# Two early loads of one column of Wa and of Wb, and a causal table that GpSimd builds behind seven of its DMA issues

## The chip, the cores and the metric

The kernel runs on one core of a Trainium2 chip. The metric is the device time of one execution in microseconds (us). Before the change it is 124.75 us, the median of three runs (124.61 to 125.31).

The core's engines are PE (matrix products), DVE (VectorE), ACT (ScalarE), POOL (GpSimd) and SP (SyncE, which here only issues DMA transfers). Each follows its own list of instructions in order, and they wait for one another by semaphores.

## The reference

Two stages follow one another. The first is a chunked state-space scan over 4 batches, 8 heads, 768 tokens, head width 32 and state width 16:

```python
cum = np.cumsum(log(a), axis=-1)                 # within a chunk of 32 tokens
L = np.exp(cum[..., :, None] - cum[..., None, :]) * causal
M = np.einsum('bhin,bhjn->bhij', C, B) * L
y = np.einsum('bhij,bhjd->bhid', M, x)           # within the chunk
y += np.einsum('bhin,bhnd->bhid', C, state) * exp(cum)
state = exp(sum(log a)) * state + sum_j(B_j x_j exp(cum_last - cum_j))
```

The second is a bilinear feed-forward layer on the result, 3072 tokens of width 256, with weights of 256 x 1536, 256 x 1536 and 1536 x 256:

```python
out = ((X @ w_a) * (X @ w_b)) @ w_out
```

## The kernel before

The kernel works with chunks of 128 tokens, six blocks of them along the sequence (`NBLK`), and takes two batches at a time. Block and batch pair give 12 **pairs** (`p` from 0 to 11). For a pair it loads B, C and x; scales B and C by the running products of `a` (`scale_bc`, giving `bm` and `cm`); turns both on PE (`transposes`); forms the scores (`scores`, into the PSUM tiles SC0 and SC1); multiplies them with a causal table of zeros and ones (`mask`, line 426 on DVE or lines 423 and 424 through ACT and POOL); multiplies the result with the scaled x (`pv_u`, line 447) and makes the state's share (`ds_mm`, line 474). The output goes to X2T (later pairs: XB), the left operand of the feed-forward layer. That layer's products with Wa and Wb go to PSUM tiles `aps` and `bps`; ACT copies `aps` to `asb` (line 639) and DVE multiplies `bps` by it into `hk` (line 646).

The order on every engine is written out by hand (`manual_schedule`): an engine does its instructions in the order in which the program's text gives them. There is no planner. PSUM banks of the feed-forward products are handed out by the string `BANKS`.

What touches the change:

- **The inputs of pair 0** are loaded first (lines 183 to 194), in pieces, alternating between SP's and ACT's DMA queues: `a`, B, C, a small table `ch`, then x. Of pair 0's x (256 KB), 192 KB go through ACT's queue and 64 KB through SP's.
- **The inputs of pair 1**: half of its x is issued by SP (`x1`, line 203), and a hand-made dependency holds this issue until DVE has made `fB` of pair 0 (line 761). B, C and the other half of x are issued by POOL (lines 215 and 218).
- **The weights** are float32 in memory and float16 on the chip, and POOL issues their transfers (`load_w`, line 171). Wa and Wb are each held in two tiles of 768 columns, `W[0]` and `W[1]`. Their first tiles come in two transfers each, one for rows 0 to 127 (`f` = 0) and one for rows 128 to 255 (`f` = 1): Wa at lines 216 and 217, Wb at 219 and 220. The second tiles follow later, one transfer for each weight.
- **The tables**: DVE fills `ident`, `causal` and `causal_q` with ones, and POOL's `affine_select` sets the unwanted elements to zero. `ident` (line 205) is the identity for the transposes. `causal` (line 210, in two halves of 64 partitions) is the mask of pairs 0 to 3, and its first reader is DVE's first masked product of pair 0 (line 426).
- **PE's first feed-forward work** is on pair 0 and comes between the parts of pair 1: three `aps` products on Wa (`units_mm`, line 628), with the scores of pair 1 in between; then four matmuls on Wb's first half, then the second product of pair 1 (line 447), its state share (line 474), and the rest on Wb (line 628). From then on whole units (`unit`, line 615) alternate with the pairs' work.

DMA issues on SP and ACT share eight completion semaphores in turn, and POOL's have eight others. An issue that takes a semaphore over waits for the transfer that used it before.

The piece of text around the change, shortened:

```python
x1 = load1(nc.sync, 1, 2, 0)
...
for w in range(2):
    for bt in range(2):
        load1(nc.gpsimd, 1, w, bt)
load_w(Wa, 0, 0)
load_w(Wa, 0, 1)
load1(nc.gpsimd, 1, 2, 1)
load_w(Wb, 0, 0)
load_w(Wb, 0, 1)
```

Of the kernel before, what the change touches and what calls it, by code (L numbers as in the profile page):

```python
# [10 lines left out]
f32 = mybir.dt.float32  # L11
# [3 lines left out]
ALU = mybir.AluOpType  # L15
# [14 lines left out]
def kernel(  # L30
# [13 lines left out]
    nc = tc.nc  # L44
# [3 lines left out]
    Q = 128  # L48
# [28 lines left out]
    causal = const.tile([128, 2, Q], f16, name="causal")  # L77
# [5 lines left out]
    big = ctx.enter_context(tc.tile_pool(name="big", bufs=1))  # L83
# [10 lines left out]
    maskbd = big.tile([128, H, D], f16, name="maskbd")  # L94
    warm = big.tile([128, 128], f16, name="warm")
    causal_q = big.tile([128, Q], f16, name="causal_q")
    Pr = big.tile([BH, NBLK, Q], f32, name="Pr")
    rmid = big.tile([BH, NBLK], f32, name="rmid")
    NE = P0 // NBP
# [43 lines left out]
    def by_token(t_):  # L143
        return t_.rearrange("p h r n -> p (h r n)").rearrange("p (t h n) -> p t h n", t=2, h=H)

    def load1(eng, p, which, bt, i0=0, n=64):
        blk, bp = divmod(p, NBP)
        if p >= P0:
            return eng.dma_start(
                by_token(pair_in[p][which])[:, bt],  # L150
                (B, C, x)[which][2 * bp + bt, :, blk * Q : (blk + 1) * Q, :].rearrange("h q n -> q h n"),
            )
        src = (B, C, x)[which][2 * bp + bt, :, blk * Q + 2 * i0 : blk * Q + 2 * i0 + 2 * n, :]
        return eng.dma_start(
            pair_in[p][which][64 * bt + i0 : 64 * bt + i0 + n].rearrange("i h r n -> i h (r n)"),
            src.rearrange("h (i r) n -> i h (r n)", r=2),
        )
# [10 lines left out]
    def load_w(W, t, f=None):  # L168
        src = (moe_w_a if W is Wa else moe_w_b).rearrange("(f p) e -> p f e", p=128)[:, :, t * KC : (t + 1) * KC]
        fs = slice(0, 2) if f is None else slice(f, f + 1)  # L170
        return nc.gpsimd.dma_start(W[t][:, fs], src[:, fs])
# [12 lines left out]
    for p_ in range(3):  # L184
# [7 lines left out]
    load1(nc.scalar, 0, 2, 1)  # L192
    load1(nc.sync, 0, 2, 0, 0, 32)
    load1(nc.scalar, 0, 2, 0, 32, 32)
    nc.scalar.preload_act_table_set("natural_log_exp_and_others")
    nc.gpsimd.memset(warm.bitcast(u32), 0)
    nc.vector.memset(ident, 1.0)
# [7 lines left out]
    nc.gpsimd.affine_select(  # L205
        out=ident, in_=ident, compare_op=ALU.is_equal, fill=0.0, base=0, pattern=[[-1, 128]], channel_multiplier=1
    )
    for bt in range(2):
        v = causal[64 * bt : 64 * bt + 64]
        nc.gpsimd.affine_select(  # L210
            out=v, in_=v, compare_op=ALU.is_ge, fill=0.0, base=0, pattern=[[-1, 2], [1, Q]], channel_multiplier=-2
        )
    for w in range(2):
        for bt in range(2):
            load1(nc.gpsimd, 1, w, bt)
    load_w(Wa, 0, 0)
    load_w(Wa, 0, 1)
    load1(nc.gpsimd, 1, 2, 1)
    load_w(Wb, 0, 0)
    load_w(Wb, 0, 1)  # L220

# [531 lines left out]
    def pull(p):  # L753
# [33 lines left out]
        out=causal_q, in_=causal_q, compare_op=ALU.is_ge, fill=0.0, base=0, pattern=[[1, Q]], channel_multiplier=-1  # L787
# [30 lines left out]
    for bt in range(2):  # L818
# [14 lines left out]
        out=hsx[0:BH],  # L833
# [246 lines left out]
```

## Time and profile before

| what | value |
|---|---|
| median of three runs | 124.75 us |
| the profiled execution's own time | 125.11 us |
| its span, from first to last instruction | 123.40 us |
| PE busy | 117.3 us, 95% |
| DVE busy | 91.0 us, 74% |
| ACT busy | 75.7 us, 61% |
| POOL busy | 61.2 us, 50% |
| moved by DMA | 12.15 MB, 99 GB/s over the span |
| granted PE clock | full in all 40 slices |

The profile is of one execution, so its span is compared with its own time: 1.71 us lie before and behind the span. A line number such as L628 is a line of the kernel before. In the timeline a row gives start, duration, engine, line, operation and tiles; consecutive instructions of one kind are merged, and "xn" counts them. Rows of DMA issues on SP, ACT and POOL say how long the issue took, not the transfer; the time from issue to landing is listed apart. The chain of waits is followed back from the last instruction: at each step to what released it.

Some landings that the text uses, in us from the span's start: `a` at 2.9; pair 0's B at 3.3 and 4.25, its C between 4.7 and 5.1, its x between 7.3 and 7.6; pair 1's B at 5.5 and 6.8, its C at 7.8 and 8.0, its x at 11.8 (SP) and 12.3 (POOL).

### The profile page before, as it was taken

How to read it: one execution, taken by the hardware profiler on the slowest of the kernel's cores; microseconds unless marked ns; L12 is line 12 of the kernel's file. 1: busy time of each engine (PE TensorE's matmuls, PEld its weight loads, DVE VectorE, ACT ScalarE, POOL GpSimd, SP SyncE). 2: the span in 40 equal slices, each digit the busy share in tenths (PEclk: the TensorE clock that was granted, in tenths of full speed). 3: DMA queues.
4: the chain of work that ended last, by engine and by line, in shares of the span. 5: the costliest groups of instructions: out<-in, count | busy, mean ns of one | idle time of the engine just before them, and what ended most of it. 6: DMA issues, size and time to landing. Idle time of an engine off the chain costs nothing.

```text
span 123.4 us, 3704 instructions
## 1 busy us (share of the span) xinstructions
PE 117.3 (95%) x1456; PEld 80.0 (65%) x1456; DVE 91.0 (74%) x182; ACT 75.7 (61%) x158; POOL 61.2 (50%) x88
## 2 busy tenths in 40 slices
PE   6799799999999999999999999999999999999990
PEld 2345669889898798744477465757464775555890
DVE  3999598973995979799986988996889544747200
ACT  0447846837669866987669767457637746657220
POOL 7997989099492994097996970056000000000000
PEclk9999999999999999999999999999999999999999
DMA  3999999978899989799977601011101012010122
GB/s 66 195 155 210 185 198 204 164 137 77 89 125 115 108 111 103 91 118 93 129 271 169 204 5 45 5 43 45 43 0 43 5 43 88 0 48 0 43 85 85
DMA packets 56401, 12.15 MB, mean 99 GB/s; under 512 B 51168, under 2 KB 55936, under 8 KB 56384
## 3 DMA queue, kind: packets, MB, share of 16 engines
q1 hardware_dynamic: 51808, 7.43, 36.3%
q0 software_dynamic: 2304, 4.06, 17.4%
q10 hardware_dynamic: 2272, 0.43, 1.8%
q8 instruction: 11, 0.18, 0.6%
q14 instruction: 6, 0.05, 0.1%
HBM read 11.13 MB, written 3.15 MB: 116 GB/s over the span
## 4 chain that ended last, share of the span: by engine, by line
PE 85%; DMA 7%; DVE 5%; issue 1%; ACT 0%; DVEq 0%
PE ops L718 17%; PE aps L693 17%; PE bps L693 16%; PE ops L661 9%; PE aps L615 8%; PE bps L615 7%; DMA Wb<-in_moe_w_b_dram 5%; PE SC L372 2%; PE SC L432 2%; PE tr L342 2%; DMA a_sb<-in_a_dram 2%; DVE hk L646 1%; PE bps L628 1%; PE SC L447 1%; PE SC L522 1%; DVE fC L246 1%
## 5 line engine op out<-in xcount | busy, mean ns | idle before, releaser
L639 ACT COPY asb<-aps 128x512 f32<-128x512 f32 x72 | 41.9, 587 | 16.0 <-PE aps L693 10.4
L703 DVE TENSOR_TENSOR hkb<-bps,asb 128x512 f16<-128x512 f32 x48 | 32.3, 688 | 11.8 <-ACT asb L639 10.4
L693 PE MATMUL aps<-XB,Wa 128*128 128x512 f16 x96 | 28.6, 379 | 0.0
L693 PE MATMUL bps<-XB,Wb 128*128 128x512 f16 x96 | 28.5, 379 | 0.0
L718 PE MATMUL ops<-Wo,hkb 128*128 128x256 f16 (+1 forms) x204 | 22.8, 267 | 0.0
L718 PEld LDWEIGHTS <-hkb 128*128 128x128 f16 x204 | 18.4, 98 | 3.0
L426 DVE TENSOR_TENSOR t<-SC,causal_q 128x512 f16<-128x512 f32 x27 | 17.3, 681 | 2.2 <-PE SC L372 2.2
L646 DVE TENSOR_TENSOR hk<-bps,asb 128x512 f16<-128x512 f32 x24 | 15.6, 681 | 3.5 <-ACT asb L639 2.1
L693 PEld LDWEIGHTS <-Wb 128*128 128x128 f16 x96 | 9.9, 103 | 11.0 <-issue 0.2
L693 PEld LDWEIGHTS <-Wa 128*128 128x128 f16 x96 | 9.7, 104 | 9.2 <-issue 0.3
L730 ACT ACTIVATE osb<-ops 128x256 f32<-128x256 f32 (+1 forms) x16 | 6.0, 376 | 12.7 <-PE ops L718 12.6
L615 PE MATMUL bps<-X2T,Wb 128*128 128x256 f16 x84 | 12.6, 273 | 0.1
L615 PE MATMUL aps<-X2T,Wa 128*128 128x256 f16 x84 | 12.5, 273 | 0.2 <-DVE hk L646 0.2
L305 POOL TENSOR_SCALAR x<-xn 128x512 f16<-128x512 f32 x8 | 11.9, 1489 | 0.7
L661 PE MATMUL ops<-Wo,hk 128*128 128x256 f16 x96 | 11.7, 273 | 0.0
L661 PEld LDWEIGHTS <-hk 128*128 128x128 f16 x96 | 9.0, 98 | 1.2
L615 PEld LDWEIGHTS <-Wb 128*128 128x128 f16 x84 | 8.5, 103 | 1.1 <-issue 0.5
L615 PEld LDWEIGHTS <-Wa 128*128 128x128 f16 x84 | 8.4, 104 | 1.2 <-issue 0.5
L424 POOL TENSOR_TENSOR t<-tmp,causal_q 128x512 f16<-128x512 f32 x5 | 5.8, 1156 | 6.2 <-ACT tmp L423 6.1
L426 DVE TENSOR_TENSOR t<-SC,causal 128x512 f16<-128x512 f32 x13 | 8.2, 678 | 0.3 <-PE SC L387 0.2
L595 POOL TENSOR_TENSOR spair<-U,ch 128x128 f16<-128x128 f32 x8 | 3.1, 398 | 10.3 <-DVE U L579 10.3
L346 ACT ACTIVATE bt<-tr,ch 128x256 f16<-128x256 f16 x16 | 6.7, 472 | 0.5 <-PE tr L342 0.5
(101 smaller groups left out, 136.1 us busy)
## 6 DMA issues: line engine op xcount, KB each, us to landing
out_dram<-osb SPq DMA_DIRECT2D x23, 128.0 KB, 1.8
xn<-in_x_dram SPq DMA_DIRECT2D x5, 256.0 KB, 4.6
cn<-in_C_dram SPq DMA_DIRECT2D x8, 128.0 KB, 4.3
bn<-in_B_dram SPq DMA_DIRECT2D x8, 128.0 KB, 4.7
Wo<-in_moe_w_out_dram POOLq DMA_DIRECT2D x2, 384.0 KB, 5.9
xn<-in_x_dram POOLq DMA_DIRECT2D x3, 256.0 KB, 4.8
Wa<-in_moe_w_a_dram POOLq DMA_DIRECT2D x2, 192.0 KB, 5.5
xn<-in_x_dram SPq DMA_DIRECT2D x3, 128.0 KB, 3.5
```

The lines of the kernel that those rows point to most:

```text
L305: eng.tensor_scalar(xo, xi, XS, None, ALU.mult)
L346: b_.append(nc.scalar.activation(out=o_, in_=TB, func=AF.Copy, scale=par[:, e : e + 1]))
L424: nc.gpsimd.tensor_tensor(out=o_, in0=tmp, in1=c_, op=ALU.mult)
L426: nc.vector.tensor_tensor(out=o_, in0=i_, in1=c_, op=ALU.mult)
L615: nc.tensor.matmul(ps[:, kk * 2 * Q : (kk + 1) * 2 * Q], w_up(W, k, f), X2T[:, p, :, f], start=(f == 0), stop=(f == 1), skip_group_check=True,
L639: (nc.vector.tensor_copy if on_dve else nc.scalar.copy)(asb, a_ps)
L646: nc.vector.tensor_tensor(out=s["hk"][:, 2 * k2 : 2 * k2 + 2, :].rearrange("p k q -> p (k q)"), in0=b_ps, in1=asb, op=ALU.mult)
L661: nc.tensor.matmul(o_ps[:, 0:d_model], hk[:, k, bt * Q : (bt + 1) * Q], Wo[:, k, :], start=(k == 0), stop=(k == NK - 1), skip_group_check= ...
L693: nc.tensor.matmul(t_, w_up(W, k, f), XB[:, blk - P0 // NBP, f].rearrange("p t j q -> p (t j q)"), start=(f == 0), stop=(f == 1), skip_gro ...
L703: return lambda: nc.vector.tensor_tensor(out=s["hk"][:, k], in0=ps[1], in1=asb, op=ALU.mult)
L718: nc.tensor.matmul(o_ps[:, 0:w], hk[:, k, c * Q : (c + 1) * Q], Wo[:, k, cs], start=(k == 0), stop=(k == NK - 1), skip_group_check=True,)
L730: nc.scalar.activation(out=o_sb[:, 0:w], in_=o_ps[:, 0:w], func=AF.Copy, scale=1.0 / (YS * YS))
```

## The change

Two things are changed, both before the first product. A new tile `first` of 128 x 2 float32 takes column 0 of rows 0 to 127 of Wa and of Wb, one element a partition, in two transfers on SP's queue; they stand behind the last piece of pair 0's x and ahead of the first x of pair 1. Nothing reads the tile. And the two `affine_select` operations that finish `causal` move down POOL's list: they stood ahead of its first DMA issue, and now stand behind the issues of pair 1's B and C, of Wa's first tile and of pair 1's x, and ahead of those of Wb.

```diff
+    first = big.tile([128, 2], f32, name="first")
...
     load1(nc.sync, 0, 2, 0, 0, 32)
     load1(nc.scalar, 0, 2, 0, 32, 32)
+    for t_, W in enumerate((moe_w_a, moe_w_b)):
+        nc.sync.dma_start(first[:, t_ : t_ + 1], W[0:128, 0:1])
     nc.scalar.preload_act_table_set("natural_log_exp_and_others")
...
-    for bt in range(2):
-        v = causal[64 * bt : 64 * bt + 64]
-        nc.gpsimd.affine_select(
-            out=v, in_=v, compare_op=ALU.is_ge, fill=0.0, base=0, pattern=[[-1, 2], [1, Q]], channel_multiplier=-2
-        )
     for w in range(2):
         for bt in range(2):
             load1(nc.gpsimd, 1, w, bt)
     load_w(Wa, 0, 0)
     load_w(Wa, 0, 1)
     load1(nc.gpsimd, 1, 2, 1)
+    for bt in range(2):
+        v = causal[64 * bt : 64 * bt + 64]
+        nc.gpsimd.affine_select(
+            out=v, in_=v, compare_op=ALU.is_ge, fill=0.0, base=0, pattern=[[-1, 2], [1, Q]], channel_multiplier=-2
+        )
     load_w(Wb, 0, 0)
     load_w(Wb, 0, 1)
```

## The prediction

> **What bounds the kernel now.** I read the page's engine rows first: PE is busy 95% of the span, DVE 74%, ACT 61%, POOL 50%, and the granted clock is full in every slice. A change that adds no matmul can then only win where PE stands still, so I looked next at where the chain of waits leaves PE. From 0 to 17 us it reads (start, us, what; whole lines, others left out):
>
> ```profile
> 2.98 0.42 DVE Pr L236
> ...
> 6.36 0.44 DVE ct L358
> ...
> 6.91 6.16 DMA Wb<-in_moe_w_b_dram
> 13.07 0.05 issue
> 13.12 0.62 PE bps L628 x4
> 13.73 0.35 PE SC L447 x32
> ...
> 15.05 0.69 DVE hk L646
> ...
> 16.12 0.69 DVE hk L646
> ```
>
> The reader is to see one transfer in it, the first half of Wb: issued by POOL at 6.91, landed at 13.07, and PE's first Wb matmul starts at once. From 16.85 on the chain is PE almost alone, so what is won or lost before that point stays to the end. The table of waits gives the size of the hole:
>
> ```profile
> PE bps L628 <- DMA Wb<-in_moe_w_b_dram: 0.7, 1, 0.7
> PEld L628 <- DMA Wa<-in_moe_w_a_dram: 0.3, 1, 0.3
> ACT x L303 <- DMA xn<-in_x_dram: 0.8, 1, 0.8
> ```
>
> Third, POOL's timeline shows what stands ahead of that issue:
>
> ```profile
> 1.40 0.87 POOL L210 TENSOR_SCALAR_AFFINE_SELECT causal<-causal 64x256 f16<-64x256 f16 x2
> 2.21 1.57 POOL L154 DMA_DIRECT2D bn<-in_B_dram  x2
> 3.77 1.37 POOL L154 DMA_DIRECT2D cn<-in_C_dram  x2
> 5.12 1.14 POOL L171 DMA_DIRECT2D Wa<-in_moe_w_a_dram  x2
> 6.20 0.77 POOL L154 DMA_DIRECT2D xn<-in_x_dram  x1
> 6.91 1.13 POOL L171 DMA_DIRECT2D Wb<-in_moe_w_b_dram  x2
> ```
>
> Fourth, the table of stretches; of its columns the last two count here, the DMA engines' busy share (it can pass 1, packets overlap) and GB/s:
>
> ```profile
> 3.00:4.00 1.00, 1.00 (x4) 0.34 (x3) 0.90 (x4) 0.00 (x0) 1.00 (x3) 1.00 0.70 110
> 6.00:8.00 2.00, 1.79 (x47) 1.12 (x47) 1.75 (x6) 1.12 (x3) 2.00 (x4) 1.00 0.97 123
> 11.00:12.00 1.00, 0.98 (x9) 0.68 (x9) 0.93 (x2) 0.58 (x1) 0.26 (x2) 1.00 1.16 212
> 12.00:13.00 1.00, 0.41 (x4) 0.12 (x2) 1.00 (x3) 0.99 (x2) 1.00 (x2) 1.00 1.23 157
> 13.00:14.00 1.00, 0.88 (x46) 0.67 (x47) 0.76 (x3) 1.00 (x3) 1.00 (x2) 1.00 1.04 193
> ```
>
> There is room before 4 us and next to none after. Bytes flow slowly twice: at 6 to 8 and at 12 to 13. The trace's packet records show why. A weight packet takes 135 ns at the median, but 20 of the 47 that start from 6.4 to 7.7 take over 250 (up to 1109), and five from 12.0 to 12.7 take 1133 to 1365; of the 459 from 12.7 to 16.7, mostly the second column halves of the same rows, one passes 250. So the slow packets look like first visits to the rows of a weight. That reading is mine; it is what the tiny loads would act on.
>
> **The change, part by part.**
>
> 1. POOL's moved selects. Seven DMA issues (four of B and C, two of Wa, one of x) stand before the new place, and all start 2.21 - 1.40 = 0.81 us sooner. The selects then run from 6.91 - 0.81 = 6.10 to 6.97, and Wb's issue stays at 6.91. What Wb gains is thus only a shorter line ahead of it in POOL's queue, whose landings follow one another: Wa's halves at 10.2 and 11.5, x at 12.3, Wb's at 13.07 and 14.07. Bounds: 0, if the engines are full anyway, and 0.81, if the whole line slides. What can really be filled is idle time: the 30% left in the stretch from 3 to 4, where the moved packets would begin (first ones now at 4.10). I take that: 0.30 us.
>
>    At its new time the first issue stands beside DVE's memsets, which run until 1.78. The trace's row: POOL's issues of this kind took 0.69 to 0.87 us, the longest of them (2.21 to 3.08) while DVE did nothing until 2.98, so none shows DVE holding it up. The Trainium skill (SBUF — State Buffer, "SBUF: two separate sides") says that GpSimd can't write a DMA's descriptors while DVE runs an operation of a two-port mode, since the two share a port pair under an exclusive lock. By that rule, if the memsets are of such a kind, the issues would gain 0.43 us and not 0.81, this term would be 0.30 x 0.43 / 0.81 = 0.16, and the sum below 0.23; no run here shows it.
>
> 2. The selects' new place. DVE's first masked product reaches its wait for the table at 7.36 and starts at 7.42; the table is ready at 6.97. Nothing, with 0.39 us of cover. Without the cover every us late costs one on DVE, less the spare of point 5. Queued behind the selects are Wb's issues, at their old time, and POOL's bm of pair 1 at 8.11.
>
> 3. The tiny loads, on SP's queue. Each has 128 pieces of 4 bytes; the nearest row is the load of ch, 128 of 40 bytes: 0.45 us of SP to issue, 11 ns a packet, 3.0 us to land. In the built program the first waits for a transfer that lands at 4.25, the second for one that lands at 4.66, so SP is done at about 5.15. Behind them is x of pair 1, which waits until 5.18 for DVE's fB in any case: hidden, and at most some 0.1 us late, where that x has 12.49 - 11.80 = 0.69 us to spare. On the DMA engines 2 x 128 x 11 ns / 16 = 0.18 us; at the busy shares above 1, where packets overlap, 0.18 / 1.15 = 0.15 us on the line ahead of Wb. Bounds: 0, and 1.1 us if each engine's first one is as slow as the slow packets.
>
> 4. What they may save. For Wa nothing: after part 1 its own packets start at about 6.46 - 0.81 = 5.65, and the tiny ones, issued from 4.25, stand in SP's queue behind x of pair 0, which is moving until about 6.5. For Wb they are in time by 5 us. Its slow second moved 157 GB/s between neighbours of 212 and 193, so it lost 1 - 157 / 202.5 = 0.22 us. Bounds: 0, and 0.95 us, by the stretch from 6 to 8 with 123 GB/s beside 234 after it (2 x (1 - 123 / 234)), though that one also has smaller packets in it. I take 0.22.
>
> 5. What is late next. If Wb came at any time, pair 1's second product would start not at 13.66 but at about 13.0: DVE's three masks of pair 1 and POOL's one end at 12.96, and ACT's scaled x, which follows the first Wa eviction, at 13.12 less the 0.18 us by which PE no longer waits for Wa's second half (its last matmul on the first half starts at 11.28, the next could at 11.39 and did at 11.57). So at most 13.66 - 13.0 = 0.66 us can be won, and as much lateness in pair 0's part is absorbed while Wb rules. The second half of Wb (14.07) is read at 14.56 and is no limit up to there.
>
> 6. Placement. The built program puts the new tile in front of others, and the B, C and x tiles start 32 bytes further, off a multiple of 64. No row shows a price. If each packet cost one row more (128 B take 13 ns, 64 B 11), 15%, pair 5's B, the tightest late load, would land 2 us after its 35.6; POOL's product would end at about 38.3 instead of 36.9, and PE turns it at 39.1. Nothing.
>
> Sum: 0.30 + 0.22 - 0.15 = 0.37, say **0.4 us less**. The profiled execution took 125.11 us (span 123.40 and 1.71 around it) and would take 124.7; it stands 0.36 above the runs' median of 124.75, from which the same step gives **124.35 us**.
>
> **The rivals.**
>
> *Full win.* The line slides by its 0.81 us, or the first visits cost more than I take; Wb lands before 12.4 and part 5 sets the end: 124.75 - 0.66 = 124.1. For it: HW queues are thin from 7 to 8 (the share is 0.81 there), so a shift need not be eaten. Against: shares of 1.03 to 1.14 from 4 to 7.
>
> *Hidden anyway.* From 8 us on the engines run full, the tiny packets take what the early start gives, and Wb's slow packets have another cause: 124.75. For it: slow packets also stand at 65 to 67 us, on x.
>
> *Slower: x of pair 0 is crowded out.* Place: the two x loads of pair 0 on ACT's queue, landed at 7.49 and 7.64. ACT's scaling waits for them (0.85 us, to 7.71), and the first product of pair 0 at 8.68 follows; it could stand 0.1 us more, since DVE's second mask ends at 8.71. The weights' packets, slow first visits among them, now come 0.8 us sooner, while more of x is still moving. Price: x lands 4.1 us after its issue at 3.58. Pair 1's first x, which moved among weights, took 6.6; at that, x lands at 10.18, 2.4 us past its time, and 0.66 of it is absorbed: 126.5. Halfway (5.35 us after issue, 8.93) it is 1.2 - 0.66 = 0.5 slower: 125.3. It decides from a landing after 7.74 + 0.66 = 8.4. For it: the row just told. Against: pair 1's B and C are out of the way sooner by as much. The Trainium skill (DMA: Bandwidth & Descriptors, "Queues, rings and completion order") says that each DMA engine goes round between the queues at packet granularity. By that rule a weight packet of 135 ns gets as many turns as x's small ones of 18, and this rival would be the result, 125.3 to 126.5; the trace agrees only in part, since x of pair 1 at 8.5 to 9.0 still moved 245 packets beside 41.
>
> That the change doesn't do what it says holds for half of it: the touch of Wa comes too late, and is counted at nothing.
>
> **How the numbers follow.** Forecast (0.15 to 0.55 won) 0.37; full win 0.25; hidden 0.17; crowded out 0.21. The range reaches from 123.95 (full win and 0.15 more, if pair 1's masks also start sooner: DVE waited 0.20 us for their scores) to 125.3 (crowded out, halfway); it leaves out the worse half of that rival and a little below. About 0.5%, 0.62 us, is what a measurement of this kernel can tell from no change. Faster by more needs the full win, nearly all of it: 0.25. Slower by more is most of the crowding: 0.17. Within: 0.58.
>
> **What would show it.** Right: POOL's first DMA issue at 1.40 and Wb's still at 6.91; the selects done by about 7.0 and no wait of DVE for POOL; Wb's first half landing at 12.5 to 12.8; no packet of Wb over 1 us; PE's wait at L628 for Wb cut from 0.7 to about 0.3. Wrong: x of pair 0 landing after 8.4 with ACT waiting for it longer than 0.85 us; a DVE wait on the table at 7.4; SP's tiny loads holding x of pair 1 past 12.5; or Wb landing at 13.07 as before.

## The result and the profile after

The changed kernel takes **126.4 us**, the median of six runs (125.8 to 127.65), against 124.91 us for the kernel before beside it. The ratio is 1.0117, with a 95% interval of 1.0078 to 1.0157. It is slower, by 1.5 us, outside the forecast range of 123.95 to 125.3. Two of the six runs, 126.90 and 127.65 us, had a granted clock of 0.984 and 0.973 and the other four 0.997 or more; the median of those four is 125.98 us, 0.9% above the kernel before. The profiled execution took 126.65 us with a span of 124.94 us; before it was 125.11 and 123.38. This execution is the slowest of those four, so that what its profile loses is more than the usual loss.

I read the chain of waits of the changed kernel first, up to 20 us (start, us, what):

```profile
2.22 3.88 DMA cn<-in_C_dram
...
6.17 0.72 DVE cm L319
6.90 0.54 DVE Pr L239
...
8.39 2.48 DVE t L429 x4
...
12.00 1.88 DVE t L429 x3
...
13.93 0.42 PE SC L450 x32
...
16.07 0.25 PE bps L618
16.32 1.36 issue
17.68 0.51 PE bps L618 x3
```

The reader is to see that Wb is gone from the chain. In its place stands pair 0's **C**, which landed at 6.09 (before 5.10). Behind it DVE's `cm` and its scan (`Pr`) are longer than they were. The first masked product starts at 8.39 instead of 7.42. Pair 1's second product starts at 13.93 instead of 13.66; Wb had landed at 13.02. Then PE halts for 1.36 us on nothing that the profile shows ("issue").

Two rows of the stretches say that the transfers are not fewer but slower. This is the changed kernel; the last two columns are the DMA engines' busy share and GB/s:

```profile
5.00:6.00 1.00, 1.00 (x6) 0.20 (x3) 0.68 (x2) 0.54 (x1) 1.00 (x2) 1.00 1.10 123
```

And this is the kernel with only the selects moved (told below), in which the DMA issues of pairs 0 and 1 stand at the same times up to 5.3 us, but for a part of x that is issued at 3.33 instead of 3.56:

```profile
5.00:6.00 1.00, 0.84 (x6) 0.17 (x3) 0.94 (x3) 0.54 (x1) 1.00 (x2) 1.00 1.08 238
```

The engines are as busy, and half as many bytes pass. The larger part is the same kind of packet in both, x's 256 bytes: 365 of them start in this stretch in the changed kernel and 708 in the other. The table of queues shows the same over the whole span (packets, MB, share of the 16 engines), first before, then after:

```profile
q1 hardware_dynamic: 51808, 7.43, 36.3%
...
q10 hardware_dynamic: 2272, 0.43, 1.8%
```

```profile
q1 hardware_dynamic: 52096, 7.43, 39.6%
...
q10 hardware_dynamic: 2272, 0.43, 2.1%
```

Queue 10 is ACT's: the same packets and bytes, and a sixth more time. In the packet records, x's packets of 256 bytes that start before 9 us took 19 ns on the mean in the kernel before and 28 (queue 10) and 35 (queue 1) in the changed one. Packets of 128 bytes in that time took 13 ns in both.

What differs about x is where it lands. The B, C and x tiles lay on multiples of 256 bytes in each partition, and the new tile `first` in front of them moves them by 32.

### The profile page after: what moved, and what is told of

It is laid out like the page before. It is cut to its first block, busy times and chain, and to the rows that moved or that the text cites. A ratio compares the mean times of both kernels' runs of the same rounds, so it can differ in the third digit from the quotient of the medians.

```text
span 124.9 us, 3706 instructions
## 1 busy us (share of the span) xinstructions
PE 117.8 (94%) x1456; PEld 80.3 (64%) x1456; DVE 91.9 (74%) x182; ACT 75.7 (61%) x158; POOL 61.4 (49%) x88
## 4 chain that ended last, share of the span: by engine, by line
PE 85%; DVE 7%; DMA 3%; issue 1%; ACTq 1%; ACT 0%; DVEq 0%
PE ops L721 17%; PE aps L696 17%; PE bps L696 16%; PE ops L664 9%; PE aps L618 8%; PE bps L618 8%; DVE t L429 4%; DMA cn<-in_C_dram 3%; PE SC L375 2%; PE SC L435 2%; PE tr L345 2%; ACTq L155 1%; DVE Pr L239 1%; PE SC L390 1%; PE SC L450 1%
## 5 line engine op out<-in xcount | busy, mean ns | idle before, releaser
L642 ACT COPY asb<-aps 128x512 f32<-128x512 f32 x72 | 41.9, 588 | 16.4 <-PE aps L696 10.3
L618 PE MATMUL bps<-X2T,Wb 128*128 128x256 f16 x84 | 12.6, 273 | 1.4 <-issue 1.4
L733 ACT ACTIVATE osb<-ops 128x256 f32<-128x256 f32 (+1 forms) x16 | 6.0, 378 | 12.7 <-PE ops L721 12.6
L308 POOL TENSOR_SCALAR x<-xn 128x512 f16<-128x512 f32 x8 | 11.9, 1489 | 0.7
L598 POOL TENSOR_TENSOR spair<-U,ch 128x128 f16<-128x128 f32 x8 | 3.1, 397 | 10.3 <-DVE U L582 10.3
```

The lines of the kernel that those rows point to most:

```text
L308: eng.tensor_scalar(xo, xi, XS, None, ALU.mult)
L618: nc.tensor.matmul(ps[:, kk * 2 * Q : (kk + 1) * 2 * Q], w_up(W, k, f), X2T[:, p, :, f], start=(f == 0), stop=(f == 1), skip_group_check=True,
L642: (nc.vector.tensor_copy if on_dve else nc.scalar.copy)(asb, a_ps)
L733: nc.scalar.activation(out=o_sb[:, 0:w], in_=o_ps[:, 0:w], func=AF.Copy, scale=1.0 / (YS * YS))
```

## The experiments

All ratios are to the kernel before, run beside each kernel (the experiments in five rounds, 6 to 12 runs each), with 95% intervals. The packet columns are means over x's packets of 256 bytes that start before 9 us, "first mask" is the start of DVE's first masked product, and "end gap" is the time from the end of PE's drain, 0.05 us after its last matmul, to its next instruction. These three columns come from one profiled execution each: the kernel with the tiny loads late has the start of the kernel before, and its first mask still stands 0.33 us later.

| kernel | ratio | x packets q10, q1 | first mask | end gap |
|---|---|---|---|---|
| before | 1 | 19, 19 ns | 7.42 us | 2.18 us |
| the whole change | 1.0117 [1.0078, 1.0157] | 28, 35 | 8.39 | 2.56 |
| selects moved alone | 0.9988 [0.9965, 1.0011] | 18, 18 | 7.60 | 2.18 |
| tiny loads alone, tile in place | 1.0047 [1.0021, 1.0072] | 30, 39 | 7.99 | 2.56 |
| the tile's room alone | 1.0033 [1.0009, 1.0058] | 29, 27 | 7.96 | 2.18 |
| whole change, tile last | 1.0024 [0.9999, 1.0048] | 18, 18 | 7.62 | 2.56 |
| whole change, tile of 64 bytes | 1.0093 [1.0070, 1.0116] | 34, 29 | 8.40 | 2.56 |
| inputs alone shifted | 1.0053 [1.0033, 1.0072] | 28, 25 | 7.80 | 2.19 |
| other tiles alone shifted | 1.0006 [0.9987, 1.0026] | 18, 20 | 7.39 | 2.20 |
| tiny loads alone, tile last | 1.0050 [1.0025, 1.0074] | 18, 20 | 7.42 | 2.56 |
| tiny loads late, tile last | 1.0016 [0.9996, 1.0036] | 21, 19 | 7.75 | 2.55 |
| eight tiny loads, tile last | 0.9978 [0.9962, 0.9994] | 18, 18 | 7.46 | 2.18 |
| whole change, 84 matmuls | 1.0112 [1.0065, 1.0159] | 33, 30 | 8.39 | 2.56 |
| selects moved, 84 matmuls | 0.9994 [0.9972, 1.0016] | 18, 18 | 7.60 | 2.18 |
| selects moved and room | 1.0087 [1.0057, 1.0116] | 29, 33 | 8.04 | 2.20 |
| whole change, memsets | 1.0077 [1.0049, 1.0105] | 33, 36 | 8.26 | 2.57 |
| whole change, eight tiny loads | 1.0062 [1.0042, 1.0081] | 32, 33 | 8.40 | 2.19 |

### First round: the parts

My first theory (A) was the slower rival of the prediction: the moved selects start POOL's loads early, and these crowd out pair 0. Against it stood the tiny loads (B) and the shift of the tiles (C).

The selects alone (the second half of the change's diff):

> The two selects behind seven of POOL's DMA issues, no tiny loads, no new tile. Theory A (the earlier start of POOL's loads crowds out pair 0's C, and the selects then run beside DVE's scaling of C): all of the loss is here. C of pair 0 lands near 6.1 us instead of 5.1, DVE's first masked product starts at about 8.4 instead of 7.42, and the ratio to the kernel before is 1.009 to 1.015. Theory B (the tiny loads hold up SP's queue and the engines): the first masked product starts below 7.6 and the ratio is 0.995 to 1.001. Theory C (the 32 bytes by which the tiles move): as B. PE's hole at the first unit's Wb product (0.27 us before, 1.36 after) is 1.2 or more if it follows from the early start, and below 0.5 if not.

The tiny loads alone (the first half of the diff):

> The two tiny loads and their tile, with the selects ahead of POOL's loads as in the kernel before. Theory A: C of pair 0 lands at 5.1 to 5.3 us, the first masked product starts at 7.4 to 7.6, and the ratio is 0.997 to 1.002. Theory B: 1.005 or more, with x of pair 0 or of pair 1 landing over 0.5 us later than before. The touch of Wb, if it works, shows as no packet of Wb over 1 us and Wb's first half landing up to 0.2 us earlier than 13.07.

The tile's room alone:

```diff
+    first = big.tile([128, 2], f32, name="first")
```

> The kernel before with the new tile's room alone: no loads, selects as before, but the B, C, x and output tiles 32 bytes further, off a multiple of 64. Theory C: packets of 64 to 256 bytes take longer on the mean, the inputs' queues use about 39% instead of 36% of the span, and the ratio is 1.003 or more. Theories A and B: ratio 0.998 to 1.002, SP's queue at 36%, C of pair 0 at 5.1 us.

The whole change with the tile behind all other tiles, so that nothing shifts:

```diff
-    first = big.tile([128, 2], f32, name="first")
...
     outp = ctx.enter_context(tc.tile_pool(name="outp", bufs=2 * P0 + 2))
+    tiny = ctx.enter_context(tc.tile_pool(name="tiny", bufs=1))
+    first = tiny.tile([128, 2], f32, name="first")
```

> The whole change, with the tiny loads' tile in a pool behind all others, so that no other tile moves. Theory A: as the changed kernel, ratio 1.008 to 1.016 to the kernel before, first masked product at about 8.4 us. Theory C: clearly less than the changed kernel, 1.000 to 1.006.

The crowding theory fell as a cost: with the selects alone pair 0's C did land later (5.66 us, before 5.10), but its last x at 7.35 (before 7.64), and the ratio is 0.9988. Room that nothing writes costs 0.3%, and taking the shift out of the whole change brings 0.9% back (1.0024; 0.6% by the four runs at the full clock). The tiny loads seem to cost something in either place: 1.0047 with the shift, and 1.0024 against 0.9988 without, where the intervals overlap.

### Second round: which tiles, and which multiple

The whole change with a tile of 64 bytes:

```diff
-    first = big.tile([128, 2], f32, name="first")
+    first = big.tile([128, 16], f32, name="first")
```

> The whole change with the new tile made 64 bytes wide (16 columns, of which two are loaded), so that the B, C, x and output tiles move by 64 bytes: a multiple of 64 again, but not of 256. Theory C1 (what counts is a start off a multiple of 64): x packets of 256 bytes take 18 to 19 ns in the first 9 us, the ratio is 1.000 to 1.005 as with the tile behind all others (1.0024). Theory C2 (what counts is a start off a multiple of 256, so that a packet crosses such a line): x packets at 28 to 35 ns as in the changed kernel and a ratio of 1.008 to 1.015.

The kernel before with only the input tiles 32 bytes further, and the tiles behind them where they were:

```diff
+    room = big.tile([128, 8], f32, name="room")
...
     inp = ctx.enter_context(tc.tile_pool(name="inp", bufs=9))
+    gap = ctx.enter_context(tc.tile_pool(name="gap", bufs=1))
+    room2 = gap.tile([128, 56], f32, name="room2")
```

> The kernel before with the B, C and x tiles alone 32 bytes further, by a room of 32 bytes ahead of their pool and one of 224 behind it; no tiny loads, selects ahead of POOL's loads. Theory C3 (the loss of the room-only kernel comes from the input transfers): ratio 1.002 to 1.005, x packets at 27 ns or more, C of pair 0 landing at 5.4 us or later. Theory C4 (it comes from the tiles behind the inputs, the scaled ones and the outputs): ratio 0.998 to 1.001.

The reverse, only the tiles behind the inputs shifted:

```diff
     inp = ctx.enter_context(tc.tile_pool(name="inp", bufs=9))
+    gap = ctx.enter_context(tc.tile_pool(name="gap", bufs=1))
+    room2 = gap.tile([128, 8], f32, name="room2")
```

> The mirror of it: the B, C and x tiles stay, and every tile behind them, the output tiles among them, moves by 32 bytes. C3: ratio 0.998 to 1.001, x packets at 18 to 19 ns; output packets of 1024 bytes may go from 46.6 to 52 ns at no cost in time. C4: 1.002 to 1.005.

The tiny loads alone, with the tile behind all others:

> The two tiny loads alone, their tile behind all others, so no tile moves; selects ahead of POOL's loads. If the tiny loads cost as such: ratio 1.001 to 1.004 (the whole change with the tile last had 1.0024, the selects alone 0.9988). If they do nothing: 0.998 to 1.001. If the touch of Wb works: Wb's first half lands before 12.9 us, no packet of it over 1 us.

It is the inputs (1.0053, against 1.0006 for the tiles behind them), and 64 is not enough (1.0093). The packets agree in every kernel of the table: 18 to 21 ns where the inputs lie on multiples of 256, 25 to 39 ns where they don't. The Trainium skill (DMA: Bandwidth & Descriptors, "How a descriptor splits into AXI transactions") has a descriptor split into transactions of 256 bytes that start on multiples of 256, and tells this of reading. Here the source did not move and the address written to did, so the rows show a like cost on the writing side; what happens inside no run here shows. A piece that crosses a multiple of 256 is not the whole of it: with the shift, every second 128-byte piece of B and C crosses one too, and these packets stayed at 13 ns.

With the selects in their old place the shift does not cost its time at the start. In the two kernels that shift the inputs and change no DMA issue (the tile's room alone, inputs alone shifted) PE starts its work behind the second `hk` 0.06 and 0.18 us earlier than in the kernel before. Both lose at 21.7 us, where PE waits 0.32 and 0.49 us for POOL's `cm` of a later pair: the last part of its C landed at 20.91 and 20.96, before at 18.99. The chain of waits with the inputs alone shifted:

```profile
15.33 5.63 DMA cn<-in_C_dram
...
21.09 0.63 POOL cm L319
21.72 0.04 issue
21.77 0.28 PE SC L345 x2
```

The tiny loads at the place without a shift still cost 0.5%, although the start looks like that of the kernel before (first mask 7.42). That left the end of the program.

### Third round: the end, and PE's halt

Of SP's waits at the end, those for the last stores are these, in the kernel before and in the changed one (us in total, times, longest):

```profile
SPq L1075 <- DMA out_dram<-osb: 1.4, 3, 0.7
```

```profile
SPq L1078 <- DMA out_dram<-osb: 1.8, 2, 1.1
```

In the trace SP waits at the end for one semaphore after another in a fixed order, and each takes some 0.06 us even where the transfer is long done. Before the change the last store has the last semaphore of this order: it landed at 122.46, and SP's last wait ended at 122.51. Two more SP issues hand it an early one, so six waits come behind its landing: it landed at 123.66, and SP's last wait ended at 124.07. That is 0.36 us more.

The tiny loads late, in front of nothing, tile last:

```diff
         if p < 10:
             loads_x(p - 1, nc.sync)
+    for t_, W in enumerate((moe_w_a, moe_w_b)):
+        nc.sync.dma_start(first[:, t_ : t_ + 1], W[0:128, 0:1])
```

> The kernel before, with the two tiny loads alone, their tile behind all others, and issued on SP only behind the input loads of pairs 6 to 11, so that they touch no weight early and stand in front of nothing at the start. Theory B, the tiny loads cost at the end: all kernels with two more DMA issues on SP so far had 2.56 us instead of 2.18 between PE's last matmul and its next instruction, and in the last us SP waits for its semaphores one by one in a fixed order, about 0.06 us each; with two issues more the last store's semaphore stands six or seven places earlier in this order. Then the place of the tiny loads does not matter: the tail is 2.56 us, and the ratio to before 1.002 to 1.005, as with them early (1.005). Rival, they cost at the start (crowding at 4 to 12 us): the tail 2.56 all the same would show that it is no cost, or 2.18, and the ratio 0.998 to 1.001.

The whole change, tile last and eight columns wide, with six more of them, late:

```diff
         if p < 10:
             loads_x(p - 1, nc.sync)
+    for t_ in range(2, 8):
+        nc.sync.dma_start(first[:, t_ : t_ + 1], moe_w_a[0:128, t_ : t_ + 1])
```

> The whole change with its tile behind all others (1.0024 before), and six tiny loads more, late, behind the input loads of pairs 6 to 11: eight in all, so that the eight semaphores which SP and ACT share fall to the last stores as in the kernel before. Theory B, the order of the waits at the end: the tail goes back from 2.56 to 2.18 us, and the ratio to 0.997 to 1.001, in spite of six loads more. Rival, each tiny load costs something where it is: the tail stays at 2.56 us or grows, and the ratio is 1.0024 or more.

The end gap follows the count of issues and not their place: 2.55 with two late ones, 2.18 again with eight. The late pair's ratio (1.0016, where I expected 1.002 to 1.005) does not exclude no change; its gap of 0.38 us would be 0.3%. The early pair took 1.0050, and whether 0.2% of that is a cost at the start is open, since the intervals overlap. Six issues more made the kernel faster, 1.0024 to 0.9978, and this last kernel beats the changed one and the kernel before: **0.9978 [0.9962, 0.9994]** of the latter. Its chain of waits shows what the change was for:

```profile
9.99 0.30 PE py L451 x14
...
12.27 0.63 ACT x L307
...
14.38 0.69 DVE hk L650
...
15.45 0.69 DVE hk L650
16.13 0.04 issue
16.18 0.60 PE aps L619 x4
```

Wb landed at 12.36 and is off the chain (ACT's scaled x, L307, is on it); both `hk` stand 0.67 us earlier than the 15.05 and 16.12 of the kernel before. But this profile is of an execution of 124.40 us, nearly the fastest of twelve (124.36 to 125.07), beside one of 125.11 before. The ratio stands for 0.27 us, which is what this kernel wins as a rule, and it does not tell this kernel from the one with the selects alone (0.9988).

PE's halt remained. In every profile of the first two rounds it was at weight load 227 of PE's list (three other instructions ahead of it are counted in; by loads alone it is the 224th), or hidden behind another wait, and it ended 2.2 to 2.5 us after the start of a 16 KB packet on the queue that the table of queues calls "instruction". Over all seventeen profiles it took 0.3 us or more in nine, four of these with the inputs on multiples of 256 bytes. In the chain of the kernel with the selects alone it reads:

```profile
15.61 0.24 PE bps L615
15.85 0.31 issue
16.16 0.51 PE bps L615 x3
```

The packet started at 13.77 here, at 13.78 before, and at 15.23 in the changed kernel, where PE resumed at 17.68. To move it, 81 weight loads and 81 matmuls were added ahead of everything:

```diff
-    warmup(11, SC[3])
+    warmup(8, SC[3])
+    for i in range(84):
+        m, bt = i % 4, i // 4 % 2
+        nc.tensor.matmul(
+            SC[m][64 * bt : 64 * bt + 64, 0:128],
+            warm[32 * m : 32 * m + 32, 0:64],
+            warm[32 * m : 32 * m + 32],
...
+            tile_position=(32 * m, 64 * bt),
+        )
```

In the whole change:

> The whole change, and three of the eleven warm-up matmuls at the start replaced by 84 small ones (32 rows, 64 columns of weights, 128 of data), which take about as long together: 81 weight loads and 81 matmuls more ahead of the first transposes, and the rest of PE's list unchanged. Theory F, PE halts because its next 16 KB of instructions have not come: in all ten profiles so far the hole is at weight load 227 of PE's list or hidden, whatever came before. Then it moves to the new load 227, which is the old 146, the first one of Wb, where PE waits for Wb anyway; PE does not stop between 15.5 and 18 us for anything but DVE; of the changed kernel's 1.36 us most are back, and the ratio to before is 1.000 to 1.006 instead of 1.0117. Rival, the halt belongs to that product (its tile, its PSUM bank, the transfers of Wb): it stays at the new load 308, the ratio 1.010 to 1.014.

In the kernel with the selects moved:

> The selects moved alone, no tiny loads (0.9988 before), with the same 84 small matmuls. Theory F: its hole at the old load 227 (0.30 us, up to 16.15) goes, what the earlier Wb wins (first half at 12.86 instead of 13.07, hk 0.2 us sooner) is no longer given back, and the ratio is 0.995 to 0.998; this would be faster than both kernels. It is spoiled if the fetch then comes later than Wb (a hole at the first Wb product behind 12.9). Rival, the halt belongs to the product: the hole stays at 16.1, ratio 0.998 to 1.001.

The halt at the old place is gone in both, and the packet started early (9.73 and 8.45 us, with PE at its load 146 in both, counted alike): it goes by the count of instructions, as the theory had it. The halt itself was not seen at its new place, where PE waits for Wb in any case. The Trainium skill (Runtime: NRT & Kernel Launch, "Instruction fetch mechanics") tells of blocks of 16 KiB, 256 instructions, fetched over the engine's own DMA queue and mostly hidden; size and queue agree, and here it was not hidden.

But the time did not follow: 1.0112 and 0.9994, where I expected 1.000 to 1.006 and 0.995 to 0.998. In the first of the two, another lateness took the place of the halt (chain of waits, then a row of the table of waits):

```profile
6.39 7.42 DMA xn<-in_x_dram
...
13.90 0.09 ACT x L306
...
17.80 0.60 PE aps L618 x4
```

```profile
PEld L631 <- DMA Wb<-in_moe_w_b_dram: 1.2, 1, 1.2
```

Pair 1's x landed at 13.8 (12.6 in the changed kernel) and Wb at 14.0. Its parts on the 16 engines were done from 11.1 to 13.8, so some engines were far behind others. Whether the early packet caused that is not shown.

### Fourth round: what the parts do together

The parts of the first two rounds did not add up: 0.9988, 1.0033 and 1.0050 against 1.0117. In the changed kernel DVE's `cm` and scan ran while POOL ran the moved selects. First POOL, then DVE (start, duration), and last the same two operations of DVE in the kernel before:

```profile
6.13 1.03 POOL L219 TENSOR_SCALAR_AFFINE_SELECT causal<-causal 64x256 f16<-64x256 f16 x2
```

```profile
6.17 0.72 DVE L319 TENSOR_TENSOR cm<-cn,fC 128x256 f16<-128x256 f32 x1 [0.45 <-DMA cn<-in_C_dram]
6.82 0.62 DVE L239 TENSOR_TENSOR_SCAN Pr<-a_sb,zero 32x128 f32<-32x128 f32 x1
```

```profile
5.56 0.42 DVE L316 TENSOR_TENSOR cm<-cn,fC 128x256 f16<-128x256 f32 x1
5.90 0.41 DVE L236 TENSOR_TENSOR_SCAN Pr<-a_sb,zero 32x128 f32<-32x128 f32 x1
```

The selects moved and the tile's room, no tiny loads (the selects' half of the diff and the line of the tile):

> The kernel before with the selects moved (0.9988 alone) and only the new tile's room in its place, so that the input tiles start 32 bytes further (1.0033 alone); no tiny loads. Theory D, the two work on one another: C of pair 0 comes later because of the shift, DVE's cm and scan then fall under the moved selects and take about 0.7 and 0.6 us instead of 0.42 and 0.41, and DVE's first masked product starts at 8.2 to 8.4 us; the ratio is 1.006 to 1.009, that is the whole change (1.0117) less the 0.003 to 0.0046 of the tail. Rival, the parts only add: 1.001 to 1.004, and what is left of the whole change's loss needs the tiny loads at the start.

The whole change with memsets in place of the selects (it leaves out the ones of the causal table, so its output is not the reference's):

```diff
-    for bt in range(2):
-        v = causal[64 * bt : 64 * bt + 64]
-        nc.gpsimd.affine_select(
-            out=v, in_=v, compare_op=ALU.is_ge, fill=0.0, base=0, pattern=[[-1, 2], [1, Q]], channel_multiplier=-2
-        )
+    for bt in (0, 0, 1, 1):
+        nc.gpsimd.memset(causal[64 * bt : 64 * bt + 64], 0.0)
```

> The whole change with its two selects replaced by four memsets of the same halves of the table (two for each), which write but do not read; the table holds zeros only, so all masked products of pairs 0 to 3 are zero. Theory L, POOL's selects hold up DVE's cm and scan because they run at the same time: cm and scan go back from 0.72 and 0.62 us to about 0.42 and 0.41, DVE's first masked product from 8.39 to about 7.9, and the ratio falls from 1.0117 to 1.005 to 1.009. Rival, cm and scan are long because DMA writes into the same memory, or because of the shifted tiles: they stay at 0.6 to 0.7, the first masked product at 8.3 or later, and the ratio at 1.010 to 1.013.

The whole change with its tile in place and six late tiny loads:

> The whole change with six late tiny loads more behind the inputs of pairs 6 to 11, as in the run with eight tiny loads (0.9978), but with the tile in its place, so that the inputs stay shifted. Between that run and this one only the tile's place differs. If placement is the main loss and the tail a second, separate one: the tail is 2.18 us as before, and the ratio 1.006 to 1.009. If the six loads healed something else than the tail in the earlier run, the ratio is below 1.004 here; if they only help where nothing else is late, it stays at 1.010 to 1.013 with the tail at 2.18.

The parts work on one another: selects and room, without tiny loads, cost 0.87%, as forecast, where the selects alone cost nothing and the room alone 0.3%. But it was not by the road of my theory D. In that kernel `cm` took 0.42 us, not 0.7, and the first mask stands at 8.04, not at 8.2 to 8.4, and only 0.08 us later than with the room alone; what its profile loses is a halt of PE of 0.96 us. With memsets, DVE's rows are short again, though POOL is as busy (6.14 to 7.60):

```profile
6.39 0.43 DVE L316 TENSOR_TENSOR cm<-cn,fC 128x256 f16<-128x256 f32 x1 [0.79 <-DMA cn<-in_C_dram]
6.73 0.40 DVE L236 TENSOR_TENSOR_SCAN Pr<-a_sb,zero 32x128 f32<-32x128 f32 x1
```

So it was the selects, and by 0.51 us (0.72 + 0.62 against 0.43 + 0.40). The Trainium skill (SBUF — State Buffer, "SBUF: two separate sides") says that a DVE operation with two SBUF inputs and a GpSimd operation that reads SBUF lock each other out for a whole instruction. The trace agrees: the selects read and delayed, the memsets only write and did not. It also shows the other side: with selects and room `cm` and the first select start together at 6.13, `cm` keeps its 0.42 us, and the two selects take 1.16 us instead of 0.87. What the lock is worth in time is not shown: 1.0077 and 1.0117 have overlapping intervals, and the first mask came at 8.26 with memsets, where I expected 7.9, since C landed 0.2 us later in that run.

The end is a separate loss: with eight loads the whole change takes 1.0062 instead of 1.0117. Four kernels now differ only in the tile's place and in the six late loads: 0.9978 with neither loss, 1.0062 with the shift, 1.0024 with the two-load end, 1.0117 with both. The two losses, 0.0084 and 0.0046, added to 0.9978 give 1.0108, within the interval of the whole change.

## Why the prediction was wrong, point by point

**The step that failed** is point 6, "Placement": "No row shows a price", and so "Nothing". It asked what a shifted packet costs the late loads of pair 5 and took 15% of a packet. For their packets of 64 bytes that was about right: 10.9 ns before, 11.9 to 13.4 in three kernels with shifted inputs. It did not ask about x's packets of 256 bytes, which the shift makes 30 to 100% longer, in the stretch where the engines run full. The shift alone brought pair 0's C at 5.8 us instead of 5.10 and its x at 8.3 instead of 7.64, and the C that PE waited for at 21.7 was not that of pair 5 either. The pairs of kernels that differ only in the shift give its price with the selects moved: 1.0087 - 0.9988 and 1.0062 - 0.9978, that is 0.99 and 0.84%, or 1.2 and 1.0 us; the third pair, 1.0117 - 1.0024, says 0.93% (0.6% by the four runs at the full clock). With the selects in their old place it costs 0.3 to 0.5%, and next to the early tiny loads nothing that shows (1.0047 and 1.0050).

**Point 3** is the second term that was missing. It priced the tiny loads on SP's queue and the DMA engines and left out the end of the program. The end gap grows by 0.38 us with them, and the ratio falls by 0.0046 without the shift where six more loads take this away; with the shift it falls by 0.0055, or by 0.002 against the four runs at the full clock. At the start SP was not done by 5.15: the second tiny load was issued at 5.69, since the first waits for a part of pair 0's C (the forecast had given this wait to the second), which landed at 5.28 instead of 4.66, and pair 1's x followed at 6.24 instead of 5.21. It landed 0.8 us later than before, about what it had to spare.

**Point 2** counted on 0.39 us of cover. With C late, the selects met not DVE's mask but the `cm` ahead of it, and made `cm` and the scan 0.51 us longer. The wait that I priced (DVE's mask on the table) never came.

**Point 1** is borne out as far as single profiles go. POOL's first DMA issue starts at 1.43 and takes its 0.87 us beside DVE's memsets, so the lock rule weighed there took nothing here. Wb's issue stands at 7.12, 0.2 us later than forecast, because the selects take 1.03 us at their new time and not 0.87. Where the inputs are not shifted, Wb's first half landed at 12.36 to 12.86 us in the four kernels with the selects moved (12.61 on the mean) and at 12.67 to 13.12 in the four with the selects in their old place (12.94). The means differ by 0.33 us, and the ranges overlap. The term was 0.30.

**Point 4** is not borne out. Slow Wb packets of over 1 us were the sign of a first visit. The kernel with only the other tiles shifted touches no weight early and has none between 10.3 and 14 us (longest 682 ns); the one with eight tiny loads has thirteen over 250 ns (longest 993). The whole change with the tile last, which does touch, has one of 1013. They come and go without the touch.

**Point 5**, the cap of 0.66 us, is met to 0.01: with Wb out of the way, in the kernel with eight tiny loads, pair 1's second product starts at 13.00, as worked out there, and both `hk` stand 0.67 us earlier. That is one fast execution, and not the usual case. The same 0.66 also absorbed most of the lateness: the first masked product is 0.97 us late in the changed kernel, the second product of pair 1 only 0.27.

The sum of 0.37 us is what the two moves are worth if nothing shifts and the end stays as it was: 0.9978 is 0.27 us, with an interval of 0.07 to 0.47. That it fits is in part luck: its term of 0.22 from point 4 is not borne out, and the sum without it, 0.15, would lie in the interval too.

**The rivals.** The slower one came in sign and in size, and x of pair 0 did land at 8.43, past its point of 8.4. That was luck: its cause was not the one named, since the earlier weight loads alone left x at 7.35, and by its own reckoning a landing at 8.43 would cost next to nothing. *Hidden anyway* fits the selects alone.

**What stays open.** In the profiled execution the changed kernel's 1.56 us more go to three places. The second `hk` ends 0.25 us later (17.05 instead of 16.80), because of the inputs. PE's last matmul ends 1.19 us later (121.73 instead of 120.54); the 0.94 between the two is the halt, which cost the kernel before nothing, since PE then waited for that `hk` in any case. The end gap is the last 0.38. But the halt is not the same in each kernel with a shift and moved selects (0.41 to 1.36 us), and moving it away did not shorten the kernel, since transfers came later in that run. It also stands in kernels without a shift (0.72 us in the whole change with the tile last, 0.54 with the other tiles shifted). So it is shown that the shift and the end make up the loss, but not by which road the shift does: how much is the halt and how much late transfers is not settled, nor why the shift costs up to three times as much with the selects moved. The lock can be a part of it in the changed kernel, but hardly with selects and room, where `cm` kept its time and the scan alone took 0.2 us more. That the halt grows with the backlog of transfers is a guess.

## What to carry to other kernels

Before pricing a new tile, list which tiles it moves and whether loads of 256-byte rows write to them: keep those on multiples of 256 bytes (32 and 64 bytes past one both cost time here), or put the new tile behind everything. Count DMA issues to the end of the program as well, since the semaphores they take in turn decide where the last store stands in the final row of waits. And when an operation is moved to another engine slot, look at what runs beside it when its neighbour is late, not only at who waits for its result.

## What the runs showed of the hardware

- x's packets of 256 bytes, beside the weights' traffic: 18 to 21 ns where the tile lies on a multiple of 256 bytes, 25 to 39 ns at 32 or 64 bytes past it. Packets of 128 bytes that start before 9 us: 13 ns in either case.
- PE stops at a fixed place of its list until 2.2 to 2.5 us after a 16 KB packet of instructions has started. The packet started at PE's weight load 143 at the earliest and at load 220 at the latest (counted with three other instructions); with 81 loads and 81 matmuls put ahead it started at load 146, 5.3 and 5.5 us sooner.
- A semaphore wait of SP at the end takes about 0.06 us though its transfer is long done; six of them made 0.36 us of an end gap that grew by 0.38.
- A POOL select on SBUF that started 0.04 us ahead lengthened DVE's two-input product from 0.42 to 0.72 us and its scan from 0.41 to 0.62; a POOL memset at the same time did not. Where the product started together with the selects, it kept its 0.42 us and the selects went from 0.87 to 1.16.
